# Matrix products of a Strassen-like scheme combined by another chain, with steps on other engines and in a new order

## The chip, the cores and the metric

The kernel runs on one core of one Trainium2 chip. The metric is the device time of one execution in microseconds (us). Five engines matter here: TensorE (in the profile PE, its weight loads PEld), VectorE (DVE), ScalarE (ACT), GpSimd (POOL) and SyncE (SP), which issues every DMA. Each engine works through its own queue in order and waits on semaphores for the others.

## What is computed

An attention read in two directions (tokens read a small state, the state reads the tokens) feeds a two-layer perceptron with softplus between its layers, all in float32:

```python
B, H, S, Ns, D = 8, 8, 512, 32, 64
scores = scale * x @ state^T           # per batch and head
a  = softmax(scores, -1);  xread = a @ state
a2 = softmax(scores^T, -1); sread = a2 @ x
x = concat([xread, sread]) -> (B*(S+Ns), H*D) = (4608, 512)
h = x @ w_in                           # (512, 2048)
g = max(h, 0) + log1p(exp(-abs(h)))    # softplus
out = g @ w_out                        # (2048, 512)
```

## The kernel before

**Rooms.** All tiles come from a few sets of equal buffers, and the profile names a tile after its set: `s` holds 512 words a partition (18 of them), `d` 1024 (14), `g` 2048 (8), `v` small ones, `b` the eight PSUM banks. `W` and `ST` are the first layer's weights and the state.

**Precision.** A float32 product is made of three products of a high and a low part: a step casts the high part (`cast`, on ScalarE, VectorE or GpSimd), a step subtracts it to leave the low part (`elementwise`, on VectorE or GpSimd).

**Blocks.** The work runs batch by batch. Batches 0 and 1 take the plain second product (`gemm2`, step `G`). Batches 2 to 7 and the state's rows (index 8) take a scheme of seven products per block (a 2 by 2 split of both factors). The second-layer weights are therefore combined once into seven slabs and stored to DRAM (steps `N`, `U`, `W`, `Y`, `K`, `j`), and each batch loads 14 slab tiles of 1 MB again (`J`, `slab_load`). For a batch of the scheme the steps are: `v` (state times `W`), `h`, `l` (its high and low part); `Q` (scores); `e`, `f`, `i` (softmax along the tokens), `1` to `7` (softmax along the state, with transposes), `8`, `9` (high and low part of the result); `t`, `u`, `R`, `r`, `y`, `z`, `Z` (the state's read: transpose, copy to SBUF, product, scaling, transpose, high and low part); sixteen times `g` (`gemm1`, six matmuls) and `s` (softplus); `F` (`form_sum`: sums of blocks of the left factor), `H`, `L` (`form_hi`, `form_lo`); fourteen times `M` (`form_product`, line 835; the seven forms in the order of `FORMS`, each in two halves); `k` (`chain`, line 866: adds each finished product from its bank to running sums), `q` (`fold`, halves added) and `P` (`fold_store`).

**Order.** `PLAN` is one character per step, in the order in which the whole program is written out; each engine's queue keeps that order (`Ordered`). `ENG` gives, for those step kinds that may run on several engines, the engine of each occurrence: A is ScalarE, D VectorE, P GpSimd. For the batches 4 and 5 the order repeats.

**What sets the order around the change.** `s_read` (`R`, TensorE) gives a bank that `s_scale` (`r`, line 553, VectorE) multiplies into the small tile `v`; `s_back` (`y`, line 564, TensorE) transposes that. `y` stands in TensorE's queue between two products `M`; all products behind it wait with it. In the repeated block of before, VectorE's queue from the last `g` on holds `F`, `L`, `e`, `k`, `1`, `2`, `3`, `6`, `7` and then `r`.

The lists that name the combination are `FORMS` (line 36), `READS` (832), `CHAIN` (861) and `ENDS` (864). In `CHAIN` an entry without a source is a copy from the bank (`cast`, on ScalarE or VectorE), an entry with one is a VectorE sum of a tile and the bank.

Of the kernel before, what the change touches and what calls it, by code (L numbers as in the profile page):

```python
# [56 lines left out]
ENG = {
    '3': "PPPDPDPDDPDPDPDP",
    '6': "PDPPDPPDDPDPDPDP",
    '8': "APAADDAAADADADADAD",  # L60
    '9': "PPDDDDDDDPDPDPDPDP",
    'D': "PDPAAAADPDPPDAAA",
    'E': "DDDDDDDDDDDPPDDD",
    'F': "DDDDPPDDDDDPDDPPDDDPDDPPDDDPDDPPDDDPDDPPPDDDDDPDDDPDDDPP",
    'H': "PADPAADPAPAAAAAADPDADAADAAAAAADPDADAADAAAAAADPDADAADAAAAAADPDADAADAAADADAAPDPDAAAAPPAAAAAAADADAPAD",
    'I': "ggggggggggdddddg",
    'L': "PDPDPDDDPDPDDDDDDPDPPDDPPDDPDDDPDPPDDPPDDPDDDPDPPDDPPDDPDDDPDPPDDPPDDDDPDPDDDPDDPPDDPDPDPDDPPDPPPP",
    'N': "PPPPDPDPPDPDPDDD",
    'O': "ggggggdgggdggddd",
    'U': "DPPPDDPD",  # L70
    'W': "ADDAAAPD",
    'Y': "DDDDDDPD",
    'h': "AAAAAAAADAAAAAADDDAAAAADAADAAAAAADDAAAAADADAAAAADADAAAAADADAAAAAADAD",
    'k': "AAADADDDDDDDDDDDDDDDDDDAADADDDDDDDDDDDDDDDDDDAADADDDDDDDDDDDDDDDDDDAADADDDDDDDDDDDDDDDDDDAADADDDDDDDDDDDDDDDDDADAADADADDDDDDDDDDDDDDDDDDDDDDDDD",
    'm': "PPPPPPPPPAPPAAPPPPPAAAAPPAPAAAAA",
    'n': "PPDDDPDPDPPPDDPPPDDPDDDDPDPDDDDP",
    'o': "DAADDAAA",
    'q': "PPPPPPPDPDPPPPPDPDPPPPPDPDPPPPPDPDPPPPDDPDDPPPPPPDDD",
    'u': "AAAADDAAAAAAAAAA",
    'w': "AAAAAAAPADPDPDPD",  # L80
    'x': "DPDPPDPDDDPDPDPP",
    'z': "AAAAAAAA",
}


# [58 lines left out]
def attention_then_softplus_mlp(ctx: ExitStack, tc, xn, xt, zq, zp, stk, w_in, w_out, out):  # L144
    nc = Ordered(tc) if PIN else tc.nc
# [571 lines left out]
    def slab_sums():  # L717
        for k in range(NFT // 2):
            w0, w1 = wsum[k], wsum[k + NFT // 2]
            t = slab[k] = r4.take([P, 4, 256], uses=2)  # L720
# [8 lines left out]
            yield
# [255 lines left out]
```

## Time and profile before

| what | value |
|---|---|
| time, median of 3 runs | 688.37 us (688.12 to 688.48) |
| the profiled execution's own time | 689.26 us |
| its span in the trace | 687.5 us |
| granted TensorE clock, mean | 0.967 |
| TensorE busy | 631.7 us |
| VectorE busy | 541.0 us |
| ScalarE busy | 303.4 us |
| GpSimd busy | 335.1 us |

The span is what the trace covers; the times of the views count from its start. A row of a list reads: line, engine, operation, output tile<-input tiles, shape and type, count | busy us, mean ns of one | idle time of the engine before it and what ended it. All steps are recorded by one helper, so every line is L99 and the tiles tell the steps apart.

### The profile page before, as it was taken

How to read it: one execution, taken by the hardware profiler on the slowest of the kernel's cores; microseconds unless marked ns; L12 is line 12 of the kernel's file. 1: busy time of each engine (PE TensorE's matmuls, PEld its weight loads, DVE VectorE, ACT ScalarE, POOL GpSimd, SP SyncE). 2: the span in 40 equal slices, each digit the busy share in tenths (PEclk: the TensorE clock that was granted, in tenths of full speed). 3: DMA queues.
4: the chain of work that ended last, by engine and by line, in shares of the span. 5: the costliest groups of instructions: out<-in, count | busy, mean ns of one | idle time of the engine just before them, and what ended most of it. 6: DMA issues, size and time to landing. Idle time of an engine off the chain costs nothing.

```text
span 687.5 us, 10638 instructions
## 1 busy us (share of the span) xinstructions
PE 631.7 (92%) x4072; PEld 496.7 (72%) x4072; DVE 541.0 (79%) x705; ACT 303.4 (44%) x464; POOL 335.1 (49%) x222
## 2 busy tenths in 40 slices
PE   3798899999999999996999699996999779999897
PEld 1476567678878887885788577784778657898686
DVE  5889969998679965798569965798569966089995
ACT  4798649624284415361354315361255314325110
POOL 2433624794338340873238530773228622079664
PEclk9899999999999999998999989998999989999999
DMA  8987444644542995378708574377807635104654
GB/s 316 406 352 257 107 154 140 223 161 155 197 199 94 417 367 195 132 298 317 295 1 335 224 291 191 122 307 300 297 15 293 259 138 224 68 1 151 217 195 142
DMA packets 48050, 146.96 MB, mean 214 GB/s; under 512 B 4224, under 2 KB 28288, under 8 KB 37248
## 3 DMA queue, kind: packets, MB, share of 16 engines
q1 hardware_dynamic: 48000, 146.29, 57.3%
q8 instruction: 32, 0.52, 0.3%
q14 instruction: 18, 0.15, 0.1%
HBM read 122.68 MB, written 23.59 MB: 213 GB/s over the span
## 4 chain that ended last, share of the span: by engine, by line
PE 62%; DVE 30%; issue 4%; ACT 3%; DMA 1%; SPq 0%; POOL 0%; DVEq 0%; ACTq 0%
PE b L99 62%; DVE d L99 10%; DVE s L99 9%; DVE g L99 6%; DVE v L99 4%; ACT s L99 1%; ACT L99 1%; DMA g<-in_w_in_dram 1%; DVE W L99 1%; ACT d L99 0%; SPq L99 0%; POOL s L99 0%; DVEq L99 0%; ACTq L99 0%
## 5 line engine op out<-in xcount | busy, mean ns | idle before, releaser
L99 PE MATMUL b<-g,d 128*128 128x512 f32 x1344 | 264.0, 351 | 7.4 <-DVE s L99 6.9
L99 PEld LDWEIGHTS b<-g,d 128*128 128x128 f32 x1344 | 214.7, 196 | 51.5 <-issue 14.6
L99 PE MATMUL b<-d,d 128*128 128x512 f32 x768 | 187.6, 397 | 5.3 <-DVE d L99 5.2
L99 PEld LDWEIGHTS b<-d,d 128*128 128x128 f32 x768 | 144.7, 191 | 48.7 <-issue 9.2
L99 PE MATMUL b<-g,s 128*128 128x512 f32 x496 | 126.1, 388 | 4.5 <-ACT g L99 2.7
L99 PEld LDWEIGHTS b<-g,s 128*128 128x128 f32 x496 | 89.5, 191 | 28.6 <-issue 6.1
L99 DVE TENSOR_TENSOR s<-s,b 128x512 f32<-128x512 f32 x117 | 73.2, 680 | 37.9 <-PE b L99 37.9
L99 POOL TENSOR_TENSOR d<-g,d 128x1024 fp32r<-128x1024 f32 x32 | 95.3, 2988 | 9.9 <-DVE d L99 5.0
L99 ACT ACTIVATE g<-b 128x512 f32<-128x512 f32 x96 | 57.2, 598 | 70.5 <-PE b L99 62.1
L99 ACT ACT_TABLE_LOAD x41 | 52.6, 1283 | 49.2 <-DVE v L99 25.3
L99 DVE TENSOR_TENSOR d<-g,d 128x1024 fp32r<-128x1024 f32 x40 | 73.7, 1847 | 0.3
L99 POOL TENSOR_TENSOR s<-s 128x256 f32<-128x256 f32 x37 | 28.6, 791 | 77.1 <-DVE s L99 73.2
L99 ACT CAST d<-b 128x512 fp32r<-128x512 f32 (+2 forms) x52 | 26.8, 558 | 56.8 <-PE b L99 56.8
L99 POOL TENSOR_SCALAR d<-g 128x1024 fp32r<-128x1024 f32 x9 | 13.2, 1468 | 75.3 <-PE b L99 68.8
L99 ACT CAST d<-g 128x1024 fp32r<-128x1024 f32 x39 | 41.0, 1051 | 19.4 <-PE b L99 12.8
L99 POOL TENSOR_TENSOR s<-s,v 128x512 f32<-128x512 f32 x18 | 21.2, 1179 | 55.3 <-DVE v L99 49.0
L99 POOL TENSOR_TENSOR g<-g,g 128x1024 f32<-128x1024 f32 x13 | 35.2, 2708 | 19.9 <-ACT g L99 7.4
L99 PE MATMUL b<-W,ST 64*32 64x512 f32 (+2 forms) x544 | 37.9, 592 | 7.4 <-DVE W L99 4.6
L99 DVE TENSOR_TENSOR d<-b,d 128x512 fp32r<-128x512 f32 (+2 forms) x68 | 41.4, 651 | 1.6 <-ACT d L99 1.5
L99 DVE CAST d<-g 128x1024 fp32r<-128x1024 f32 x24 | 30.5, 1278 | 11.0 <-PE b L99 11.0
L99 POOL TENSOR_SCALAR s<-s 128x512 fp32r<-128x512 f32 x19 | 15.5, 814 | 39.5 <-PE b L99 13.6
L99 DVE TENSOR_TENSOR g<-g 128x1024 f32<-128x1024 f32 x10 | 31.5, 3189 | 0.0
(86 smaller groups left out, 688.9 us busy)
## 6 DMA issues: line engine op xcount, KB each, us to landing
g<-slabs SPq DMA_DIRECT2D x84, 1024.0 KB, 6.9
d<-in_xt_dram SPq DMA_DIRECT2D x16, 512.0 KB, 6.0
d<-in_xn_dram SPq DMA_DIRECT2D x16, 512.0 KB, 5.9
slabs<-d SPq DMA_DIRECT2D x16, 512.0 KB, 2.9
slabs<-g SPq DMA_DIRECT2D x24, 256.0 KB, 5.8
out_dram<-s SPq DMA_DIRECT2D x48, 128.0 KB, 2.0
g<-in_w_in_dram SPq DMA_DIRECT2D x11, 512.0 KB, 9.7
g<-in_w_out_dram SPq DMA_DIRECT2D x11, 512.0 KB, 9.9
```

The source lines that it names most:

```text
L99: return lambda *a, **k: self.tc.keep_in_program_order(f(*a, **k))
```

## The change

The seven products run in another order of forms, and they are combined in another chain. Each half of a batch's rows (index p) had nine sums with a bank and two copies; it has seven sums and one copy. The difference of the form 7, `Sf`, is still made first, but used fifth; one slab changes its sign. The sums of the left factor are made at other forms. The engine lists are new: all 98 `L` are on VectorE (56 before, 42 were on GpSimd), 81 of 98 `H` on ScalarE (60 before), 8 on GpSimd (13 before), 42 of 56 `F` on VectorE (37 before); of `m` and `n`, high and low part of the plain product, 7 and 3 of 32 stay on GpSimd (19 and 14 before); `N`, `U`, `W`, `Y` leave GpSimd but for one `N`. And `PLAN` is another order throughout. In the repeated block, VectorE's and TensorE's steps from the last `g` to `y` were `M H H L F Q M F e e 1 M k 1 k L M i H i 2 2 3 M k k k k L M 5 6 5 t 7 t k M k L 7 M L R k k M r q y` (with copies on ScalarE among the `k`), and are now `M F L Q F M e e L M F 1 1 M H L L M M k k L t q k t M k L L M i i L L R k M k r L 2 2 y`.

```diff
-FORMS = (7, 1, 4, 2, 5, 6, 3)
+FORMS = (1, 2, 6, 5, 7, 3, 4)
 SLAB = {5: 0, 6: 1, 7: 2, 4: 3, 1: 4, 2: 5, 3: 6}
 PLAN = (
...
-    "65t7JLtukMukL67MJHLRJHkkMqrqLPPyM88Jz99ZvJkkMhkhkllMJvJkkMqhkhqPkPkqkqPMlTlPJgJkkqvqsPgPhlhglsgTsgsFvsHghhLgsl"
-    "lgsgsFgsHHgsLgsLgsHFgLsgsgsMsHHHFLFQJHLMFXXeef1MJLk1kfLFMiJHHiw22F3MJkkkkHL34MxJHL5465tJLtwkMukuL67x7wMJHxLRwJ"
...
+    "vsLghhlglsgsgsHgsLgsgFsgsHgsLgsgFsFMsHFLQJFMeHefLMXFJkXkF1f1HMHJHLHFLMJHMHkJkqLPtqJktuPMkHuLLMJHiiLLRHJkMkrL22"
+    "y3MJzL4Z354vJMk6hkhkqkqPlPMlJ5768vJkkMqh7hqPl8Pl9MT9TJgJkkqvqsPgPhlhglsgsgsHvsLghhlglsgsgsHgsLgsgFsgsHgsLgsgFs"
...
 ENG = {
...
-    'D': "PDPAAAADPDPPDAAA",
-    'E': "DDDDDDDDDDDPPDDD",
-    'F': "DDDDPPDDDDDPDDPPDDDPDDPPDDDPDDPPDDDPDDPPPDDDDDPDDDPDDDPP",
-    'H': "PADPAADPAPAAAAAADPDADAADAAAAAADPDADAADAAAAAADPDADAADAAAAAADPDADAADAAADADAAPDPDAAAAPPAAAAAAADADAPAD",
+    'D': "AAPDDAAAAPPDAPAD",
+    'E': "DDDDDDDDDDDDDPDD",
+    'F': "DDDDDDPDDDDDDDPDDDDDDDPPDDDDDDPPDDDDDDPPPDPDDDDDDDDDPPPP",
+    'H': "DAAAAAAAAAAAAAAAAAAADAAAAPAAAAAAAADAAAAPAAAAAAAADAAAAPAAAAAAAADAAAAPAADADDAAADAPAAAAAAAAPAAAPAAAAP",
...
-    'L': "PDPDPDDDPDPDDDDDDPDPPDDPPDDPDDDPDPPDDPPDDPDDDPDPPDDPPDDPDDDPDPPDDPPDDDDPDPDDDPDDPPDDPDPDPDDPPDPPPP",
-    'N': "PPPPDPDPPDPDPDDD",
+    'L': "DDDDDDDDDDDDDDDDDDDDDDDDDDDDDDDDDDDDDDDDDDDDDDDDDDDDDDDDDDDDDDDDDDDDDDDDDDDDDDDDDDDDDDDDDDDDDDDDDD",
+    'N': "DPDDDDDDDDDDDDDD",
...
-    'U': "DPPPDDPD",
+    'U': "DDDDDDDD",
...
-    'm': "PPPPPPPPPAPPAAPPPPPAAAAPPAPAAAAA",
-    'n': "PPDDDPDPDPPPDDPPPDDPDDDDPDPDDDDP",
+    'm': "AAAAAPPADAAPAPPDPAPAAAAAAAAAAAAA",
+    'n': "DDPDDDDDDDDDDPDDPDDDDDDDDDDDDDDD",
...
-            elementwise(t[:, 3], t[:, 1], b21, ALU.subtract, e)
+            elementwise(t[:, 3], b21, t[:, 1], ALU.subtract, e)
...
-            if f in (5, 3):
+            if f in (2, 3):
                 a12, a22 = block(b, 1, c, 0), block(b, 1, c, 1)
-            if f == 7:
+            if f == 1:
                 Sf[b, c] = r2.take([P, 4, 128], uses=2) if b == B else r4.take([P, 4, 256], uses=2)
                 elementwise(Sf[b, c].t, a11, a21, ALU.subtract, engine())
                 TT[b, 0, c].done()
-            elif f == 5:
+            elif f == 2:
                 elementwise(a21, a21, a22, ALU.add, engine())
...
-    READS = {7: 1, 1: 2, 4: 1, 2: 1, 5: 2, 6: 3, 3: 1}
+    READS = {1: 1, 2: 1, 6: 1, 5: 1, 7: 2, 3: 1, 4: 1}
...
-    CHAIN = {7: (("q", None, None),), 1: (("w", None, None), ("q", "q", ALU.add)), 4: (("v", "q", ALU.subtract),),
-             2: (("u", "w", ALU.add),), 5: (("w", "w", ALU.add), ("q", "q", ALU.add)),
-             6: (("v", "v", ALU.add), ("q", "q", ALU.add), ("w", "w", ALU.add)), 3: (("w", "w", ALU.add),)}
-    ENDS = {(2, 0): ("u", 0, 0), (6, 0): ("v", 1, 0), (6, 1): ("q", 1, 1), (3, 0): ("w", 0, 1)}
+    CHAIN = {1: (("m", None),), 2: (("c", "m"),), 6: (("m", "m"),), 5: (("v", "m"),), 7: (("x", "v"), ("m", "m")),
+             3: (("v", "v"),), 4: (("m", "m"),)}
+    ENDS = {(2, 0): ("c", 0, 0), (7, 0): ("x", 1, 1), (3, 0): ("v", 0, 1), (4, 0): ("m", 1, 0)}
...
-                                nc.vector.tensor_tensor(sums[b, p, to].t, sums[b, p, of].t, m.t, op)
+                                nc.vector.tensor_tensor(sums[b, p, to].t, sums[b, p, of].t, m.t, ALU.add)
```

## Rows read from the trace of the kernel before

**Rows 1.** The page, busy time (share of the span) and instructions of each engine.
```profile
PE 631.7 (92%) x4072; PEld 496.7 (72%) x4072; DVE 541.0 (79%) x705; ACT 303.4 (44%) x464; POOL 335.1 (49%) x222
```

**Rows 2.** Waits of TensorE, the longest: us in total, times, longest us.
```profile
PE b L99 <- DVE v L99: 21.1, 4, 5.9
PE b L99 <- DVE s L99: 6.9, 2, 4.2
```

**Rows 3.** Chain that ended last, 390 to 480 us: start, us, what.
```profile
393.97 42.80 PE b L99 x238
...
439.30 6.66 DVE g L99 x2
```

**Rows 4.** Windows, busy us by engine (instructions), then PEclk, DMA share, GB/s.
```profile
399.30:436.80 37.50, 37.50 (x223) 28.12 (x223) 21.90 (x31) 15.23 (x24) 8.25 (x7) 1.00 0.49 188
436.80:471.90 35.10, 29.25 (x236) 24.24 (x235) 33.39 (x41) 14.54 (x21) 23.85 (x11) 0.98 0.70 270
```

**Rows 5.** VectorE's groups by form, 427 to 472 us.
```profile
L99 DVE TENSOR_TENSOR d<-g,d 128x1024 fp32r<-128x1024 f32 x6 | 9.3, 1546 | 0.0
L99 DVE TENSOR_TENSOR g<-g 128x1024 f32<-128x1024 f32 x2 | 6.7, 3408 | 0.0
L99 DVE CAST d<-g 128x1024 fp32r<-128x1024 f32 x4 | 5.0, 1246 | 2.8 <-PE b L99 2.8
L99 DVE TENSOR_TENSOR s<-s,b 128x512 f32<-128x512 f32 x6 | 3.8, 674 | 0.0
...
L99 DVE STREAM_TRANSPOSE s<-b 128x512 f32<-128x512 f32 x2 | 1.4, 706 | 1.4 <-ACT s L99 1.4
...
L99 DVE TENSOR_TENSOR d<-g 128x1024 f32<-128x1024 f32 x1 | 1.2, 1225 | 1.8 <-ACT g L99 1.8
```

**Rows 6.** Timeline of VectorE, 437 to 473 us: start, us, what, count.
```profile
436.79 1.38 DVE L99 CAST d<-g 128x1024 fp32r<-128x1024 f32 x2 [2.76 <-PE b L99]
...
467.50 1.21 DVE L99 TENSOR_TENSOR d<-g,d 128x1024 fp32r<-128x1024 f32 x1
```

**Rows 7.** Windows behind TensorE's five long waits, columns as in Rows 4.
```profile
316.50:321.00 4.50, 4.42 (x16) 3.80 (x17) 3.67 (x5) 0.27 (x1) 4.08 (x3) 0.55 0.68 218
393.97:399.30 5.33, 5.33 (x17) 4.41 (x17) 3.93 (x5) 0.27 (x1) 4.10 (x2) 0.52 0.76 255
471.90:477.20 5.30, 5.30 (x17) 4.39 (x17) 3.89 (x5) 0.27 (x1) 4.09 (x2) 0.50 0.74 255
545.86:550.10 4.24, 4.24 (x14) 3.40 (x14) 4.24 (x6) 1.14 (x2) 4.02 (x3) 0.60 0.61 259
553.74:559.30 5.56, 5.56 (x23) 4.45 (x25) 3.36 (x7) 0.89 (x2) 3.62 (x3) 0.50 0.50 147
```

**Rows 8.** GpSimd's groups by form, 437 to 472 us.
```profile
L99 POOL TENSOR_TENSOR g<-g,g 128x1024 f32<-128x1024 f32 x3 | 8.2, 2733 | 3.3 <-ACT g L99 1.9 <-ACT s L99 1.4
...
L99 POOL TENSOR_TENSOR s<-s 128x256 f32<-128x256 f32 x1 | 0.7, 724 | 4.1 <-DVE s L99 4.1
```

**Rows 9.** The page, costliest groups of the whole execution.
```profile
L99 ACT ACT_TABLE_LOAD x41 | 52.6, 1283 | 49.2 <-DVE v L99 25.3
...
L99 POOL TENSOR_SCALAR d<-g 128x1024 fp32r<-128x1024 f32 x9 | 13.2, 1468 | 75.3 <-PE b L99 68.8
...
L99 ACT CAST d<-g 128x1024 fp32r<-128x1024 f32 x39 | 41.0, 1051 | 19.4 <-PE b L99 12.8
```

**Rows 10.** Windows of the first part, columns as in Rows 4.
```profile
0.00:124.00 124.00, 101.09 (x632) 70.25 (x633) 104.59 (x197) 93.74 (x140) 47.80 (x51) 0.94 0.71 251
124.00:174.00 50.00, 49.55 (x370) 38.17 (x369) 45.92 (x52) 20.58 (x35) 38.02 (x33) 1.00 0.51 172
9.00:35.00 26.00, 17.83 (x122) 10.20 (x123) 23.58 (x55) 20.92 (x45) 11.13 (x11) 0.87 1.04 404
```

**Rows 11.** Window of one whole repeated block, columns as in Rows 4.
```profile
394.70:472.40 77.70, 71.85 (x474) 56.64 (x473) 58.99 (x75) 29.83 (x47) 35.97 (x20) 0.96 0.61 230
```

**Rows 12.** Slab loads issued between 400 and 480 us.
```profile
DMA to landing us min/median/max: 4.8/6.9/12.3
```

**Rows 13.** Timeline of TensorE, 394 to 473 us; here two halves of a form.
```profile
407.21 5.92 PE L99 MATMUL b<-g,d 128*128 128x512 f32 x32
```

More of the change, by code (lines that the diff above doesn't have):

```diff
@@ new lines @@
+    "TSTISTTIIQII1IQ2Ie3OaXbfI1Ic4tO2vuOQ5hhOIla6IbI73aSc88O4e9vOa9Ohh5fatlla6ub7ac88b1919cgblcavbbgIehhlflcAgcAsbt"
+    "XBcgIBICumvCDnDEsEhGmhslsGnmBAIenGOlBfgiCAmigDsCEGDsnaEgbO2OG2a3casGb3bOgacbGBcAcmRsCvnDGBAmTEhmGrAlhnGml4nAg4"
+    "CnDgBTsEjBGCsCDBGjDmEAEgn5aGjsCt65GDujaGEbO6bOgaabOcAGjcsbGccjmBGOmBCAOnvDnjvAEhmChGhlhDAjlGllgEBjnAGsCBTgDCmE"
+    "jgDBTnsEvsCQXihDXihGlmjleEGjefG1n17gXmf7XAjBGn88CsG9j9BGiAmignjDCtsEGDuEjG223g34jGgs5jt6sGu4QojvopNeGNphhefgjl"
+    "olopUgpfm1yjtsWRzKYRZvKrs1njmuvhNGhmlhlhjGllnmgNjrUGsnGmWnKgYGNKsNnGmUgnWNvsNKYGhhlKGmlUmgnWGnsNKYGNKg5GUms6nG"
@@ new lines @@
+    "WmKgYnKGsNGNUmgnWGsKYGmKnNgGsGN7Ug8m79WGnsKG8YmJ9gKNNGsnJmUyGzZWngJYKGsKmGnJgitisGuGgGsGgGsyGz2Z32g34GsG5o6voH"
+    "pogph7hplovlsp4LghghlslgFs5gsH6gs7LgsgFsgsHFgsLgsgsMsHFLMJFFHFMXLHJkXkSHMHJLHLFMJHkkqLPMHJqLPRJHkkvLMHrLhhllMJ"
+    "HLMJkkLLyMJ8z89Z9MJkkqkPkqMPJvJkkMqhqhPlPlMTTJgJkkqvqsPgPhhlglsgsgsHvsLghhlglsgsgsHgsLgsgFsgsHgsLgsgFsFMsHFLQJ"
+    "FMeHefLMXFJkXkF1f1HMHJHLHLMJHkkqLPMHJqLPiitFJtuMkuHkLLMJHLLRJHkkMr223L4yMJz3Z455vJk6Mhkhkqk6PllqMJ7P78899vJkkM"
+    "qhqhPlPlMTTJgJkkqvqsPgPhlhglsgsgsHvsLghhlglsgsgsHgsLgsgFsgsHgsLgsgFsFMsHFLQJFMeHefLMXFJkXkF1f1HMHJHLHFLMJHMHkJ"
@@ new lines @@
+    "kqLPtqJktuPMkHuLLMJHiiLLRHJkMkrL22y3MJzL4Z354vJMk6hkhkqkqPlPMlJ5768vJkkMqh7hqPl8Pl9MT9TJgJkkqvqsPgPhlhglsgsgsH"
+    "vsLghhlglsgsgsHgsLgsgFsgsHgsLgsgFsFMsHFLQJFMeHefLMXFJkXkF1f1HMHJHLHFLMJHMHkJkqLPtqJktuPMkHuLLMJHiiLLRHJkMkrL22"
+    "y3MJzL4Z354vJMk6hkhkqkqPlPMlJ5768vJkkMqh7hqPl8Pl9MT9TJgJkkqvqsPgPhlhglsgsgsHvsLghhlglsgsgsHgsLgsgFsgsHgsLgsgFs"
+    "FMsHFLQJFMeHefLMXFJkXkF1f1HMHJHFLHwMJHkxkMHJLLqtqJtwkPMukHPuLwLMJHxiiLLRHJwkMxrkL2xyMJ2zZ334L4vJkMkhqkhPkqlPwl"
+    "Mx55v6Mh6hkkqlPlqM7P78899vkwgkqhxhPlqwgslwPxgxsgsJgswxvsghhlJglsgsgsJgsgsgsJgsgsgsgsgsgswwxxgswwxxgswwxxgswHHx"
@@ L56 @@
+    "LLgsHHLLgFFsHHLgFLsMFsHHLLFFMJFFFFHMJkkHkLLFFHMJFLHHLHHFLHMJHHkHHkFkLMJqFqPqPHLHMHPLJHkkkLLMJLHHLLLMHJHkkkLLLM"
+    "JLLLMJkkqkPkqkkqMPPMkkqkPqqMPPMkqMPkqkqPP"
 )
 ENG = {
[L58 to L61, printed above, removed]
[L62 to L65 removed]
@@ L75 @@
-    'm': "PPPPPPPPPAPPAAPPPPPAAAAPPAPAAAAA",
-    'n': "PPDDDPDPDPPPDDPPPDDPDDDDPDPDDDDP",
[L77 to L82, printed above, removed]
+    '3': "PPPPPDPDPDPDPDDD",
+    '6': "DDPPDPPDPPPPPPDD",
+    '8': "AAAAAAAAAAAAAAAAAA",
+    '9': "PPPPDDPDDDDDDDDDDD",
+    'D': "AAPDDAAAAPPDAPAD",
+    'E': "DDDDDDDDDDDDDPDD",
+    'F': "DDDDDDPDDDDDDDPDDDDDDDPPDDDDDDPPDDDDDDPPPDPDDDDDDDDDPPPP",
@@ new lines @@
+    'H': "DAAAAAAAAAAAAAAAAAAADAAAAPAAAAAAAADAAAAPAAAAAAAADAAAAPAAAAAAAADAAAAPAADADDAAADAPAAAAAAAAPAAAPAAAAP",
+    'I': "ggggggggggdgdddg",
+    'L': "DDDDDDDDDDDDDDDDDDDDDDDDDDDDDDDDDDDDDDDDDDDDDDDDDDDDDDDDDDDDDDDDDDDDDDDDDDDDDDDDDDDDDDDDDDDDDDDDDD",
+    'N': "DPDDDDDDDDDDDDDD",
+    'O': "gggggddgggddddgg",
+    'U': "DDDDDDDD",
+    'W': "DDAAAAAA",
+    'Y': "DDDDDDDD",
+    'h': "AAAAAAADDAAAAAAAAAAAAAAAAADAAAAAADAAAAAADAAAAAAADAAAAAAADAAAAAAAAAAD",
+    'k': "AADDDDDDDDDDDDDDAADDDDDDDDDDDDDDAADDDDDDDDDDDDDDAADDDDDDDDDDDDDDAADDDDDDDDDDDDDDADADDDDDDDDDDDDDDDDDDDDD",
@@ L83 @@
+    'm': "AAAAAPPADAAPAPPDPAPAAAAAAAAAAAAA",
+    'n': "DDPDDDDDDDDDDPDDPDDDDDDDDDDDDDDD",
+    'o': "DAAADAAA",
+    'q': "PDPPPDPDPDPPPDPDPDPPPPPDPDPPPPPDDDPPPPPPDDDPPPPDDDDD",
+    'u': "AAAADADAAAAAAAAA",
+    'w': "AAAPAAAPPDDDDDDD",
+    'x': "PPPPPDDDDDDDDDDD",
+    'z': "DAAAAAAA",
 }
@@ L871, in chain @@
                         m = prod[(b, p), f]
-                        for n, (to, of, op) in enumerate(CHAIN[f]):
+                        for n, (to, of) in enumerate(CHAIN[f]):
                             if of is None:
```

21 lines of the change are left out of this document (removed).

## The prediction

> **What bounds the kernel now.** First the page: TensorE is busy in 631.7 of 687.5 us [rows 1], so only 55.8 us are idle, and the question is who keeps it waiting. The list of TensorE's waits answers: four waits for the small tile `v` make up 21.1 us, and two for an `s` tile 6.9 [rows 2]; most of the rest lies in the first 110 us. A `v` tile that TensorE waits for is what `s_scale` (`r`) writes and `s_back` (`y`) transposes: one wait per batch, up to 5.9 us. The chain of waits, read in order of time, shows how a batch comes to it: 42.8 us of TensorE without a break, then pieces of VectorE up to `y`, two of them of 6.66 us together [rows 3]. So I looked at the two halves of one batch as windows. In the first, TensorE is busy in all 37.5 us and VectorE in 21.9. In the second, TensorE has 29.25 us of work in 35.1, VectorE is busy for 33.39, and GpSimd for 23.85 [rows 4]. VectorE bounds the second half, and the missing 5.85 us are the wait at `y`.
>
> Why VectorE takes 33 us there is to be seen in its groups: the same shape has several prices. A low part (`L`) of 128x1024 averages 1546 ns, while a single one takes 1.21 us; a block sum in place takes 3408 ns, one into another room 1225; a cast of 128x1024 averages 1246 ns, while two in a row take 1.38 us, 0.69 each. Sums with a bank stay at 674 [rows 5, 6]. The dear ones lie beside GpSimd work. The surplus is 6 x 0.34 + 2 x 2.18 + 4 x 0.56 = 8.6 us, against 23.85 us of GpSimd: 0.36 us lost on VectorE per us of GpSimd.
>
> A wait also costs clock. In the windows right behind the five long waits the granted clock is 0.50 to 0.60 of full speed, the 1.2 GHz level, after TensorE had stood still for 3.6 to 5.9 us; while it works on, it is 1.00 [rows 4, 7]. Length times missing clock gives 2.0 + 2.6 + 2.7 + 1.7 + 2.8 = 11.8 us of lost work [rows 7].
>
> **The change part by part.**
> TensorE gets the same matmuls, so its work stays. What may go is waiting.
>
> *The second half of a batch.* Counted from the new order and engine lists, VectorE does there, up to `r`: nine `L` at 1.21 (10.9), three block sums at 1.23 (3.7), six sums with a bank at 0.674 (4.0), one cast (0.7), two maxima and two transposes at 0.7 (2.8), and some nine small instructions, 1.5 as an estimate from the fold-sized ones: 23.6 us without a neighbour [rows 5, 6]. That is not less than before (33.4 less 8.6 is 24.8): four low parts come over from GpSimd, and the softmax along the state moves behind `y`. What goes is the neighbour. GpSimd keeps two block sums at 2.73, one fold at 0.72 and one cast at 1.47 there, 7.65 us in place of 23.85 [rows 8, 9]. At 0.36 that adds 2.8, and VectorE needs 26.4 us. TensorE needs 29.25, less some 0.7 for the last softplus: 28.5. VectorE is then ready some 2 us ahead of `y`, and the wait at `y` goes. Bounds of the block sums, now mostly on VectorE: 1.23 to 3.41 each; I take the low end, since the two on GpSimd are all that can meet them. An earlier deadline is the second half of form 6: VectorE must have done 11 us of this list (three `L`, three block sums, the softmax's first steps, a cast) by the time that TensorE has done five products and `Q`, 5 x 2.96 + 1 us [rows 13]: 4 us of room.
>
> *The chain.* Seven sums for nine, and one copy for two per index: four VectorE sums (2.7 us) and two ScalarE copies a batch. Most lie in the first half, where VectorE has slack [rows 4]; worth nothing beyond what is counted above.
>
> *Casts on ScalarE.* Three more `H` a batch at 1.05 (3.2 us) [rows 9] beside 29.8 us in 77.7 [rows 11]; ScalarE stays under half busy, so nothing. In the first part 14 more steps move to it (about 0.6 each, an estimate from the large casts, 8.7 us), but the new order changes between softplus and the other functions 36 times instead of 42: six table loads at 1.28 (7.7) less [rows 9]. Even.
>
> *What goes.* The four waits at `y`, 21.1; the two for `s` tiles, 6.9 (one beside a batch's end, one where low parts on GpSimd met the last batch's products); the clock behind five of them, 11.8. Together 39.8 us, which leaves 687.5 - 39.8 = 647.7.
>
> *The first 124 us.* VectorE is busy for 104.6 of them and sets the pace, TensorE for 101.1 [rows 10]. By the lists 25 flexible steps are on GpSimd there instead of 43, and VectorE has 47 instead of 43: about 20 of 47.8 GpSimd us less, 7 us of surplus less at 0.36, 3 us of steps more. I take 2 us of gain. The loads are in a new order, too: two more of `x^T` (512 KB each) now stand ahead of the second piece of `w_in`; at 404 GB/s [rows 10] that is 2.6 us for the products that want that piece. Bounds: 8 us either way.
>
> *124 to 174 us.* TensorE never waits there, VectorE is busy for 45.9 of 50 us and GpSimd for 38 [rows 10]. VectorE now takes 46 flexible steps instead of 33, GpSimd 4 instead of 22. Priced without a neighbour I get 44 to 49 us, about TensorE's own 49.5. This is where VectorE could become late anew: I take 2 us of loss, with 0 to 10 as bounds (the upper end if these steps keep the prices that they had beside GpSimd).
>
> *Left over.* An order written out by hand has small waits somewhere: one us in each of five batches, 0 to 4 each; the last has four more low parts of the weights on GpSimd. Plus 5.
>
> Sum: 647.7 - 2 + 2 + 5 = 652.7 us of span. The median of the runs shown is 0.87 us over the span (688.37 to 687.5), so 653.6.
>
> **The rivals.**
> 1. *GpSimd holds VectorE for the whole of each of its instructions.* Then the 7.65 us [rows 8, 9] count in full: 23.6 + 7.65 = 31.3 against 28.5, a wait of 2.8 us at `y`, plus 2.3 of clock (11.8 over five waits). Five batches give 25, of which 5 are counted; the last has 6 us more GpSimd work: 654 + 26 = 680. For it: in-place sums at 3408 [rows 5], a free one plus almost a GpSimd one. Against it: all dear instructions together lost only 0.36 per us. The Trainium skill ("SBUF — State Buffer", section "Who interferes with whom") states this rule: the pair of ports that VectorE and GpSimd share is an exclusive lock for whole instructions when VectorE has two SBUF inputs or runs in a 2-port mode. By it the sum is rival 1's; the rows agree for single instructions, and disagree with it as a price for every GpSimd us.
> 2. *VectorE becomes late in the first 174 us*, at the upper bounds: 8 + 10 in place of 0: 18 us more would be 672, half of it 663; I write 668. For it: VectorE's share there is already the highest of the kernel [rows 10].
> 3. *Slab loads become the wait, and the kernel slower.* A batch moves 230 GB/s x 77.7 us = 17.9 MB [rows 11]; without the waits it has 69.5 us, so 257 GB/s. Only four slab rooms are free, and a product takes 2.96 us [rows 13]: a load must land 3 x 2.96 = 8.9 us after its room is free. It lands in 6.9 at the median and 12.3 at worst [rows 12]. Each turn of four rooms costs what the landing has over 8.9; with 2.5 turns a batch and 5.4 batches' worth, 34.7 us are given back, and the kernel becomes slower, from an overall landing of 11.5 on. At 12.3 everywhere: 654 + 46 = 700. Against it: TensorE has no wait for a slab now, and DMA reached 404 GB/s [rows 10].
> 4. *The change doesn't do what it says:* `r` stands behind as much VectorE work as before, and the waits at `y` stay as they are: 688. Against it is the count above.
>
> **How the numbers follow.** The forecast, 646 to 662, gets 0.66; rival 1 0.12 (680), rival 2 0.10 (668), rival 3 0.07 (700), rival 4 0.03 (688), and 0.02 go to less than 640. The predicted time is 654. The range reaches down to 640 (no new wait and the first part's best bound: 647.7 - 8) and up to 682, past rivals 1 and 2. About 0.2% (1.4 us) is what a measurement of this kernel can tell from no change: faster by more 0.90, within 0.03, slower 0.07.
>
> **What would show it.** TensorE's waits should list `v` with under 4 us in all, and the page a granted clock near 1 behind 120 us. In a repeated block's second half GpSimd should be busy for about 8 us, the 128x1024 low parts should average near 1.25 us, and VectorE have idle time that ends with TensorE. Two transposes `y` should lie 70 us apart, not 77.7. Rival 1 would show as `v` waits of about 3 us with low parts above 2 us; rival 2 as waits for `s` or `d` tiles before 174 us; rival 3 as waits of PE for DMA `g<-slabs`. The prediction is wrong if a wait that isn't in the list of before, of 5 us or more per batch, takes the place of the one at `y`.

## The result and the profile after

The changed kernel takes 634.67 us (median of four runs, 634.05 to 634.82) against 688.25 for the kernel before (median of four): a ratio of 0.922, interval 0.9205 to 0.9237. The direction was forecast; the time lies 5.3 us below the low end of the range. The profiled execution took 634.05 us, its span 632.3. Of the 55 us of span that are gone, 40.8 lie where the prediction put its 39.8, behind 242 us; it was the two stretches ahead that gave 14.5 where it expected nothing.

The page's first line, to be held against [rows 1]: TensorE is busy in 97% of the span, and GpSimd does 123 us in place of 335.

```profile
PE 613.6 (97%) x4072; PEld 485.3 (77%) x4072; DVE 486.6 (77%) x741; ACT 326.8 (52%) x497; POOL 123.0 (19%) x108
...
L99 ACT ACT_TABLE_LOAD x35 | 44.9, 1283 | 2.3 <-DVE v L99 1.7
```

All of TensorE's waits (us in total, times, longest). No `v` tile is among them, where [rows 2] had 21.1 us, and no slab. All of them lie in the first 53 us:

```profile
PE b L99 <- DMA ST<-in_zp_dram: 5.0, 1, 5.0
PE b L99 <- ACT s L99: 3.3, 2, 1.9
PE b L99 <- DVE W L99: 2.7, 2, 2.0
PE b L99 <- ACT d L99: 1.8, 1, 1.8
PE b L99 <- DMA d<-in_xt_dram: 0.7, 1, 0.7
PE b L99 <- DVE g L99: 0.7, 2, 0.4
PE b L99 <- POOL d L99: 0.2, 1, 0.2
```

The chain that ended last, between 355 and 440 us, is one piece, where [rows 3] showed 42.8 us of TensorE and then VectorE up to `y`:

```profile
354.94 85.17 PE b L99 x632
```

Windows of one repeated block, `y` to `y` (columns as in [rows 4]): the two halves, and the second up to the end of `r` alone; then the whole block ([rows 11]) and the first two stretches ([rows 10]).

```profile
365.70:406.60 40.90, 40.90 (x243) 30.89 (x242) 24.92 (x37) 19.48 (x31) 6.06 (x8) 1.00 0.55 211
406.60:435.30 28.70, 28.70 (x235) 24.06 (x233) 27.62 (x35) 14.43 (x19) 8.30 (x5) 1.00 0.83 323
...
406.60:432.75 26.15, 26.15 (x219) 21.85 (x218) 25.07 (x32) 14.43 (x19) 7.55 (x4) 1.00 0.81 313
...
365.70:435.30 69.60, 69.60 (x477) 54.96 (x475) 52.54 (x72) 33.91 (x50) 14.36 (x13) 1.00 0.67 257
0.00:111.10 111.10, 96.69 (x630) 67.28 (x631) 95.83 (x202) 91.59 (x148) 25.16 (x32) 1.00 0.77 278
111.10:159.10 48.00, 48.00 (x368) 37.96 (x367) 46.71 (x83) 23.90 (x39) 4.57 (x4) 1.00 0.56 182
```

In the windows that begin at 0 the clock can read too high: the trace's first entry on it lies at 16.8 us before and at 25.9 us after, and what is ahead of it counts as 1.00. The last section shows what the matmuls tell there.

The second half shows TensorE without a gap, VectorE still busy in 27.62 of 28.7 us, and `r` done at 432.75, 2.5 us ahead of `y` at 435.3. It is the same in three of the four batches that waited. In the last one GpSimd has 14.30 us of work in the half, and `r` ends only 0.06 us ahead of `y`: there the wait is gone, and no slack is left.

```profile
476.20:504.90 28.70, 28.70 (x233) 23.84 (x231) 27.75 (x32) 15.99 (x22) 14.30 (x8) 1.00 0.85 325
```

VectorE's groups by form around it (395 to 435 us, columns as in [rows 5]): eleven low parts in place of six, and a block sum in place at 1217 ns instead of 3408.

```profile
L99 DVE TENSOR_TENSOR d<-g,d 128x1024 fp32r<-128x1024 f32 x11 | 14.9, 1366 | 7.2 <-ACT d L99 7.2
L99 DVE TENSOR_TENSOR s<-s,b 128x512 f32<-128x512 f32 x6 | 3.8, 675 | 0.0
...
L99 DVE TENSOR_TENSOR g<-g 128x1024 f32<-128x1024 f32 x2 | 2.4, 1217 | 0.0
...
L99 DVE CAST d<-g 128x1024 fp32r<-128x1024 f32 x1 | 2.0, 2042 | 0.0
```

The slab loads issued between 360 and 440 us ([rows 12] for before):

```profile
DMA to landing us min/median/max: 4.9/9.2/12.6
```

Where the 55 us went, by the starts of the eight transposes `y` in the two timelines (us from the mark before):

| mark | before | after | less |
|---|---|---|---|
| first `y` | 123.8 | 111.1 | 12.7 |
| second | 49.8 | 48.0 | 1.8 |
| third, fourth | 17.0, 51.9 | 17.0, 51.9 | 0 |
| fifth | 74.1 | 68.1 | 6.0 |
| sixth | 77.4 | 69.5 | 7.9 |
| seventh | 77.9 | 69.6 | 8.3 |
| eighth | 81.9 | 69.7 | 12.2 |
| end | 133.8 | 127.4 | 6.4 |

### The profile page after: what moved, and what is told of

It reads as the page before. It is cut to its first block, busy times and chain, and to the rows that moved or that the text cites. A ratio compares the mean times of both kernels' runs of the same rounds, so it can differ in the third digit from the quotient of the medians.

```text
span 632.3 us, 10553 instructions
## 1 busy us (share of the span) xinstructions
PE 613.6 (97%) x4072; PEld 485.3 (77%) x4072; DVE 486.6 (77%) x741; ACT 326.8 (52%) x497; POOL 123.0 (19%) x108
## 4 chain that ended last, share of the span: by engine, by line
PE 83%; DVE 1%; ACT 1%; issue 0%
PE b L99 83%; DVE s L99 1%; DVE d L99 1%; ACT L99 0%; ACT s L99 0%; DVE g L99 0%; ACT d L99 0%
## 5 line engine op out<-in xcount | busy, mean ns | idle before, releaser
L99 PE MATMUL b<-g,d 128*128 128x512 f32 x1344 | 252.1, 340 | 0.1
L99 DVE TENSOR_TENSOR d<-g,d 128x1024 fp32r<-128x1024 f32 x72 | 99.0, 1388 | 44.9 <-ACT d L99 44.5
L99 ACT ACTIVATE g<-b 128x512 f32<-128x512 f32 x96 | 57.0, 597 | 77.9 <-PE b L99 77.8
L99 ACT CAST d<-g 128x1024 fp32r<-128x1024 f32 x59 | 61.2, 1050 | 33.7 <-PE b L99 16.3
L99 DVE TENSOR_TENSOR s<-s,b 128x512 f32<-128x512 f32 x91 | 57.4, 677 | 27.2 <-PE b L99 27.2
L99 POOL TENSOR_TENSOR g<-g,g 128x1024 f32<-128x1024 f32 x10 | 25.9, 2592 | 141.6 <-DVE g L99 81.8
L99 ACT ACT_TABLE_LOAD x35 | 44.9, 1283 | 2.3 <-DVE v L99 1.7
L99 DVE TENSOR_TENSOR d<-d,d 128x1024 fp32r<-128x1024 f32 (+1 forms) x22 | 27.1, 1243 | 1.0 <-ACT d L99 0.9
L99 ACT ACTIVATE s<-b 128x512 f32<-128x512 f32 x32 | 18.6, 599 | 14.2 <-PE b L99 14.0
L99 ACT COPY s<-b 128x512 f32<-128x512 f32 x32 | 17.8, 589 | 14.8 <-PE b L99 14.6
L99 ACT CAST d<-d 128x1024 fp32r<-128x1024 f32 x18 | 18.8, 1048 | 10.6 <-DVE d L99 8.0
L99 DVE TENSOR_TENSOR s<-s,s 128x512 fp32r<-128x512 f32 x31 | 21.8, 709 | 2.4 <-ACT s L99 2.4
```

The costliest lines, as they stand in the source:

```text
L99: return lambda *a, **k: self.tc.keep_in_program_order(f(*a, **k))
```

## The experiments: the steady batches

The theory on record says that the neighbour, GpSimd, made VectorE late at `y`, and that taking its work away is what removes the wait. The rival is the order: `r` stood behind the softmax along the state, whoever worked beside it. The engine lists and the order can be changed one without the other.

**Low parts back on GpSimd, in the changed kernel.**

```diff
-    'L': "DDDDDDDDDD...",   # 98 on VectorE
+    'L': "PDPDPDDDPDPDDDDDDPDPPDDPPDDPDDDP...",   # the list of before: 42 on GpSimd
```

> The kernel after with the list L of before: 42 of the 98 low parts back on GpSimd, nothing else. Theory A (waits at y came from VectorE beside GpSimd): VectorE's second half of a batch loses four low parts (4.8 us) and gains 0.36 to 0.44 us for each of some 13 us of added GpSimd (5 us), while GpSimd's own low parts of 2.4 to 3.4 us stand in the chain to the products: waits of 0 to 4 us per batch, time 636 to 660. Rival B (the order alone removed the waits): 634 to 636, no wait of TensorE behind 35 us. If the port lock counted in full: waits of 6 us or more at y per batch, time above 665.

640.26 us, 0.9285 to 0.9312 of before: 5.6 us more than the change. The time lies low in theory A's wide range and above the 634 to 636 of rival B, so by itself it decides little. But GpSimd is as busy in the half as it was before, and still there is no wait of more than 1.3 us. The second half of a block:

```profile
411.30:440.10 28.80, 28.40 (x231) 23.55 (x230) 25.09 (x27) 14.12 (x19) 22.99 (x9) 1.00 0.77 286
```

GpSimd 22.99 us here and 23.85 in [rows 4]; the wait at `y` is gone in one and 5.85 us long in the other. The two kernels differ in order, forms, chain and the other lists; the next runs change one of these at a time.

**The same list the other way, in the kernel before.** All 98 `L` on VectorE, nothing else.

```diff
-    'L': "PDPDPDDDPDPDDDDDDPDPPDDPPDDPDDDP...",
+    'L': "DDDDDDDDDD...",
```

> The kernel before, its order and chain kept, with all 98 low parts on VectorE. Theory A: in the second half of a batch GpSimd loses 13 us and VectorE gets 4.8 us of low parts and loses 5 us of surplus: VectorE 33.4 to 33 us, the wait at y shrinks only a little unless block sums become cheaper too; I expect 660 to 685 us. Rival B (the order alone decides): the waits at y stay at 5.8 us, 686 to 692. Rival C (the engine list alone decides): the waits at y vanish, 648 to 655.

685.86 us, 0.9943 to 0.9975: some 3 us less, just between the ranges of theory A and rival B. The waits at `y` are not shorter but longer, 6.3 to 6.4 us in the three steady batches. The gain lies elsewhere: the wait of 2.7 us for an `s` tile at 650 us is gone, and from the eighth `y` to the end it takes 129.7 us in place of 133.8. TensorE's wait for `v`, and the second half:

```profile
PE b L99 <- DVE v L99: 23.5, 4, 6.4
```

```profile
437.25:472.90 35.65, 29.26 (x236) 24.25 (x235) 33.98 (x45) 14.45 (x21) 11.38 (x6) 0.98 0.64 252
```

GpSimd's work is halved and VectorE's stays at 34 us: the instructions that got cheaper (low parts at 1370 ns, block sums in place at 2313) only made room for the low parts that came over. So the list of the low parts does not remove the wait in the old order. The other lists were left as they were in this run.

**The order alone, in the kernel before.** The steps 2 to 9 of the softmax along the state go behind `r` in the three batches that repeat, all but `2` behind `y` too; forms, chain and the engine of each step kind stay.

```diff
-    ...HHi22F3MJkkkkHL34M5JHL465t7JLtukMukL67MJHLRJHkkMqrqLPPyM88Jz99ZvJkkMhkhkllMJvJkkMqhkhq...
+    ...HHiFMJkkkkHLMJHLtJLtukMukLMJHLRJHkkMqrqL22PPy3MJz4Z354vJkkM6hkhk5llM7J68vJkk7Mq8hk9hq9...
```

> The kernel before with one change of order: in the three repeated batches the softmax along the state (2, 3, 4, 5, 6, 7, twice each) and its high and low parts stand behind the transpose y, as in the kernel after, not ahead of the scaling r. Engines and chain are those of before. Theory C (the order decides: these steps put 7 to 8 us of VectorE work ahead of r, dear ones beside GpSimd included): the three waits of 5.8 us at y vanish, VectorE's second half falls from 33.4 to about 26 us, and 3 x (5.8 + 2.4 of clock) = 25 us go: 662 to 668. Theory A (GpSimd beside VectorE decides): the waits shrink by half at most, 674 to 684. Rival: another wait takes their place, 686 to 690.

664.62 us, 0.9635 to 0.9679. `y` to `y` is 68.1, 69.5 and 69.6 us: those of the changed kernel to the tenth. `r` is done 1.3 to 1.4 us ahead of `y`. Windows of the second half up to the end of `r` and up to `y`; the one up to the end of `r` in the kernel before; and VectorE's groups by form from 410 us to that `y`:

```profile
420.70:448.03 27.33, 27.33 (x226) 22.86 (x225) 25.80 (x29) 13.00 (x18) 21.36 (x9) 1.00 0.77 299
420.70:449.40 28.70, 28.70 (x234) 24.04 (x233) 27.17 (x31) 13.00 (x18) 22.73 (x9) 1.00 0.79 305
```

```profile
436.80:471.65 34.85, 29.23 (x235) 24.22 (x233) 33.14 (x40) 14.54 (x21) 23.60 (x10) 0.99 0.70 272
```

```profile
L99 DVE TENSOR_TENSOR d<-g,d 128x1024 fp32r<-128x1024 f32 x6 | 9.3, 1558 | 0.0
L99 DVE TENSOR_TENSOR g<-g 128x1024 f32<-128x1024 f32 x2 | 6.7, 3408 | 0.0
L99 DVE CAST d<-g 128x1024 fp32r<-128x1024 f32 x4 | 5.0, 1246 | 2.8 <-PE b L99 2.8
```

These are the dear prices of [rows 5], within 12 ns: the neighbour is there in full, and `r` is in time. What left the queue ahead of `r` is the softmax, 7.3 us of VectorE (33.14 to 25.80). That settles the three steady batches.

**The order alone, in all four batches that wait for `v`.** The last one, too; there the steps `w` and `x` (high and low part of `W`, for the state's rows) had to move later with it.

> The kernel before with the softmax along the state moved behind y in VectorE's queue, now in all four batches that wait for it (the last batch too, where the steps of w and x of the fourth batch move later with it). Theory of the order: the last batch's two waits before y (4.2 and 3.6 us, at 545 and 553 us) go as those of the other three went, y to y of that batch falls from 81.9 to 69.6 to 72 us, and the time to 652 to 656 us. Rival, that the last batch's waits come from its fewer rooms for other work and stay in part: y to y 75 to 82 us, time 658 to 665 us.

654.64 us, 0.9488 to 0.9518. The last batch falls from 81.9 to 69.5 us, `r` 0.55 us ahead of `y`. No `v` is left among TensorE's waits, with 20.63 us of GpSimd in its second half:

```profile
490.60:519.40 28.80, 28.80 (x234) 24.12 (x233) 27.16 (x30) 11.94 (x17) 20.63 (x7) 1.00 0.77 303
```

A new order of a few softmax steps gives 34 of the 54 us, with the chain, the lists and the first part of before.

**The chain of nine sums again, in the changed kernel.** The sums of forms 2 and 5 and the copies are issued twice, with the same result.

```diff
...
-    nc.vector.tensor_tensor(sums[b, p, to].t, sums[b, p, of].t, m.t, ALU.add)
+    for _ in range(2 if f in (2, 5) else 1):
+        nc.vector.tensor_tensor(sums[b, p, to].t, sums[b, p, of].t, m.t, ALU.add)
```

> The kernel after with nine sums and two copies per index again: the sums of forms 2 and 5 and the copy of form 1 are made twice, with the same result. All four extra sums of a batch (2.7 us of VectorE) lie ahead of r, where r is done 2.5 us before y. Theory (seven sums are worth what slack they buy): waits of 0 to 1 us per batch, 634.5 to 639. Rival (VectorE sets the pace of a batch): 2.7 us x 6.5 batches = 18, time 650 to 653.

639.04 us, 0.9272 to 0.9305: 4.4 us more. `r` ends 0.06 to 0.4 us ahead of `y`, no longer 2.5, and `v` is back among the waits with 2.0 us in all, 1.3 of them in the last batch, which had no slack. The slack that the shorter chain leaves is used nearly to its end.

**How much slack VectorE has.** The low parts of forms 5 and 6 are made twice, with the same result.

> The kernel after with the low parts of forms 5 and 6 made twice, with the same result: four more VectorE instructions of 1.2 us per batch (4.7 us) ahead of r. By the account of the second half (27.6 us busy of 28.65, r done 2.5 us before y) 3.6 us fit, and 1 to 2.2 us of wait come per batch, TensorE waiting for v or d: 640 to 648. Rival (all hidden): 634 to 636. Rival (no slack, all on the path): 4.7 x 6.5 = 31, time 660 to 668.

656.29 us, 0.9517 to 0.9551: 21.6 us more, a miss. `y` to `y` is 2.3 to 5.4 us longer in each of the four batches, most in the last one, which had no slack, and the waits are spread over three kinds of tile:

```profile
PE b L99 <- DVE v L99: 6.4, 4, 2.3
PE b L99 <- DVE d L99: 5.5, 7, 2.2
...
PE b L99 <- DVE s L99: 1.6, 1, 1.6
```

The slack of 2.5 us at `y` is not the only one: all seven waits for a `d` tile end with a low part, which a product wants soon after it is made, and each product that comes late is a wait of its own.

## The experiments: the first part

Here the forecast was 2 us of gain, and 12.7 came. The first `y` is the mark. TensorE's waits up to it, in the kernel before:

```profile
PE b L99 <- DMA ST<-in_zp_dram: 4.9, 1, 4.9
PE b L99 <- DVE d L99: 4.8, 2, 3.5
PE b L99 <- DVE W L99: 4.6, 2, 2.4
PE b L99 <- ACT d L99: 2.9, 2, 2.7
PE b L99 <- ACT g L99: 2.7, 1, 2.7
PE b L99 <- DVE g L99: 1.8, 4, 0.9
PE b L99 <- DMA d<-in_xt_dram: 1.2, 1, 1.2
```

22.9 us against 14.4 after, 8.5 of the 12.7. The rest is TensorE's own busy time, 100.89 us up to that mark against 96.69. Both changes lie behind the first loads: up to 33 us TensorE waits for 13.6 us before and 13.9 after, behind that for 9.3 and 0.4. After two of these later waits in the kernel before (2.7 us for `g`, up to 55.8 us, and 3.5 us for `d`, up to 87.2) the granted clock falls to half:

```profile
57.70:61.20 3.50, 3.50 (x10) 2.68 (x10) 3.50 (x5) 3.50 (x7) 1.59 (x1) 0.51 1.08 390
88.50:91.90 3.40, 3.40 (x10) 2.63 (x9) 1.74 (x3) 2.23 (x3) 0.00 (x0) 0.50 0.73 248
```

That is 3.4 us of lost work, and the changed kernel has no such fall behind 26 us. The stretches behind 35 us, before and after:

```profile
35.00:123.80 88.80, 80.85 (x478) 59.38 (x477) 78.76 (x138) 71.12 (x95) 34.77 (x33) 0.96 0.61 207
35.00:111.10 76.10, 75.59 (x471) 56.17 (x470) 68.65 (x141) 69.73 (x101) 19.36 (x20) 1.00 0.68 238
```

So waits and the clock behind them are 11.9 of the 12.7 us, as in the batches. What shortened the waits is the question of the runs that follow.

**The order of the first loads.** The changed kernel with two loads of `x^T` behind two pieces of `w_in`, as before; the order of the first loads is then that of before but for one load of the state.

```diff
-    "TSTISTTIIQII1IQ2I...",
+    "TSTISIITTQII1IQ2I...",
```

> The kernel after with the first loads in the order of before: the two loads of x^T of batch 1 behind the second and third piece of w_in, all else kept. Theory (the order of loads is a small part of the first part): the second product with W starts 1 to 3 us earlier (16.0 to about 14), the scores of batch 1 later, first y within 2 us of 111.1, time 633 to 637. Rival (the order of loads brought the gain): first y at 117 or later, time above 640.

635.01 us, 0.9215 to 0.9242; first `y` at 111.8, as in a second trace of the changed kernel. The loads' order, one of the prediction's worries, costs and gives nothing that shows.

**The engine lists of the first part.** First the old lists in the new order; then the new lists in the old order; then of these only the lists that divide work between GpSimd and VectorE (3, 6, 9, E and n).

> The kernel after, its order and all else kept, but the steps ahead of the first transpose y take the engines that before gave the same occurrences (3, 6, 8, 9, D, E, m, n, h, u, o): 41 of them on GpSimd instead of 24. Theory A (the first part gained 12.7 us, 123.8 to 111.1 us, because VectorE lost less time beside GpSimd, and because TensorE kept its clock without long waits): most of the gain goes, first y near 119 to 124 us, time near 643 to 648 us, VectorE's int32 shifts (TENSOR_SCALAR) back from 455 to 600 ns or more. Rival B (the gain comes from the new order of steps and loads): first y stays near 111 to 113 us, time 635 to 637.

> The kernel before, its order kept, with the engines of after for the occurrences ahead of the first y: GpSimd does 24 of these steps instead of 41. Theory A (less GpSimd beside VectorE makes the first part short): first y from 123.8 to 112 to 117 us, time 677 to 682. Rival B (order): first y stays at 121 to 124, time 685 to 688.

> The kernel before; ahead of the first y only the steps that leave GpSimd for VectorE move (lists 3, 6, 9, E, n as in after), no cast moves to ScalarE, which keeps its work and its 30 table loads of the first part. Theory D (moving casts to ScalarE made the kernel with all early lists slower, since ScalarE there was busy for 98.7 of 126.7 us): first y at 118 to 122 us, 2 to 5 us faster than before, 683 to 687. Rival (VectorE is the engine that is late, and gets more work): first y at 124 to 127, time 688 to 692.

| first `y`, us | lists of before | lists of after |
|---|---|---|
| order of before | 123.8 | 126.7 |
| order of after | 117.9 | 111.1 |

The times are 641.96, 692.16 and 686.54 us (0.9304 to 0.9337, 1.0037 to 1.0066, 0.9961 to 0.9986 of before). Each mark is read from one trace; a second trace of the changed kernel has 111.8. The third run came as its theory had it; the first two did not: 117.9 lies between the two ranges given, and 126.7 above both. The new order gives 5.9 us with the old lists. The new lists cost 2.9 us in the old order and give 6.8 in the new one; the lists of GpSimd and VectorE alone give 2.4 in the old order (first `y` at 121.4), so it is the others, most of which move steps to ScalarE, that cost there. The windows up to the first `y`, old lists in the new order, and new lists in the old order:

```profile
0.00:117.90 117.90, 98.20 (x631) 68.54 (x632) 103.31 (x195) 86.30 (x134) 45.55 (x47) 0.94 0.73 261
```

```profile
0.00:126.70 126.70, 102.17 (x631) 70.09 (x632) 97.97 (x196) 98.65 (x151) 30.15 (x34) 0.97 0.69 245
```

With the old lists VectorE is the busiest (103.31), with the new lists in the old order ScalarE is (98.65), with 29 table loads of 1283 ns before the mark. The new order has 24, with either lists. That ScalarE has the room for what the new lists give it only there is an argument so far; the runs with table loads added and taken away test it. What in the new order gives its own 5.9 us was not taken apart further, but the loads' order is not it.

**The new first part ahead of the old rest.**

> All steps up to the first y in the order and on the engines of after, all steps behind in the order, on the engines and in the chain of before. Theory (the first part stands by itself): first y at 111 to 112 us instead of 123.8, the waits at y as before, time 688.4 - 12.7 = 675 to 677. Rival (the gain of the first part is paid back by steps that it leaves for later, VectorE being busy for 46 of 50 us there): 680 to 688.

679.17 us, 0.9856 to 0.9884: 9.2 us of the 12.7, between the ranges of theory and rival. The first `y` comes at 112.2, and behind it a wait of 2.7 us shows at 121 us, where the old rest follows on the new order.

**Table loads added.** Three tiny softplus calls among other functions, which bring six more table loads, 30 before the first `y`.

```diff
+            if k in (7, 10):
+                nc.scalar.activation(probe, probe, AF.Softplus)
```

> The kernel after with three tiny softplus calls on a tile of one column, each between two calls of the other table, so that ScalarE loads a table six times more in the first part: 30 as before instead of 24, 7.7 us plus some 0.6 us for the calls. Theory E (fewer table loads gave ScalarE the room for the casts that left GpSimd): first y 4 to 8 us later, 115 to 119, time 638 to 643. Rival (ScalarE has slack there): first y at 111 to 113, time 634 to 637.

639.87 us, 0.9283 to 0.9309: 5.2 us more; first `y` at 116.4, ScalarE gets 6 x 1.283 + 3 x 0.2 = 8.3 us of work more. It has so little slack in this part that 4.6 to 5.3 of the 8.3 us arrive at TensorE, by the two traces of the changed kernel (111.8 and 111.1). That is most of the 6.8 us that the new lists give in this order.

**Table loads taken away.** Two steps moved ahead of one softplus, two ahead of another (`a` and `A`, in which ScalarE takes the upper half of a weight of `w_in` or `w_out` from its stored words; the texts on record call them low-part and copy steps): 20 loads in place of 24 before the first `y`, all the four behind 33 us. The first of these runs stood without the changed kernel beside it; the two that follow share a chip.

```diff
-...OG2a3casGb3bOgacbGBcAcmRsC...   ...CnDgBTsEjBGCsCDBGjDmEAEgn5aGjsC...
+...OG2a3caaAsGb3bOgcbGBccmRsC...   ...CnDgBTAasEjBGCsCDBGjDmEEgn5GjsC...
```

> The changed kernel with four of ScalarE's table loads less in the first part (two low-part and copy steps moved ahead of one softplus, two ahead of another), 20 in place of 24 before the first y. Theory that the loads set the length of the first part: each load is 1283 ns, and 8.3 us of added loads and work cost 5.3 us, so four less give back 0.64 x 5.1 = 3.3 us at most: first y at 108 to 110 us in place of 111.1, time 631 to 634 us. Rival, that ScalarE's slack in this part is used up only when more is added: first y 110.5 to 111.5, time 634 to 636 us.

> The changed kernel itself, so that the next one is timed on the same chip beside it: 634 to 635 us, first y at 111 us, TensorE's waits of the first part 14.4 us in all and none behind 33 us.

> The changed kernel with four table loads less, all of them behind 33 us, beside the changed kernel. TensorE of the changed kernel waits in its first part only before 33 us. Theory that a load costs only where TensorE waits or the granted clock falls: no difference beyond 0.2%, 633.0 to 635.5 us, first y at 110.5 to 111.5 us, with ScalarE some 5 us less busy before it. Rival, that the loads set the pace of the first part: 1.5 to 3.3 us faster, first y at 108 to 109.6 us.

633.58 us in the first run (0.9187 to 0.9212 of before). Side by side: 633.68 us (633.15 to 634.04) against 635.42 (634.96 to 635.96) for the changed kernel, so 1.7 us or 0.27%, with ranges that don't meet. The first `y` moves by 1.3 us, from 111.8 to 110.5. The theory of no difference beyond 0.2% missed, though its range holds the first `y`. The rival's 1.5 to 3.3 us hold the 1.7, but its 108 to 109.6 don't hold the first `y`, and the trace doesn't show loads that pace the whole part. TensorE's timeline shows the one place, 16 matmuls of a product with `W`, in the changed kernel, with four loads less, and with six more:

```profile
48.86 2.08 PE L99 MATMUL b<-W,ST 64*32 64x512 f32 x16
```

```profile
49.24 1.09 PE L99 MATMUL b<-W,ST 64*32 64x512 f32 x16
```

```profile
49.30 1.81 PE L99 MATMUL b<-W,ST 64*32 64x512 f32 x12
52.74 1.05 PE L99 MATMUL b<-W,ST 64*32 64x512 f32 x4 [1.63 <-DVE W L99]
```

The same 16 matmuls take 1.09 us with nothing to wait for. In the changed kernel they take 2.08, and the list of waits is silent: pauses shorter than a matmul's own record count as busy. They want `W` columns that VectorE makes from ScalarE's output, and in the changed kernel VectorE waits for that output just there:

```profile
48.72 1.11 DVE L99 SCALAR_TENSOR_TENSOR W<-s,s 128x512 int32<-128x512 int32 x1 [0.94 <-ACT s L99]
```

ScalarE has three loads around this point (at 44.8, 46.7 and 49.8 us), and two with four loads less (46.3 and 49.2). By the starts of the same matmuls in both kernels, the lead made here is 1.3 us (0.4 us behind at matmul 260, 1.0 ahead at 320) and changes by 0.3 in the rest of this part: the other loads are hidden. With six loads more, 2.1 us of the lag are made at the same place and most of the rest near 60 and 85 us. The version with four loads less is the fastest of the study.

## Why the prediction was right, and where it failed

- **The waits at `y`, the `s` tiles and the clock behind them (39.8 us):** right in size. From the fourth `y` to the end the marks give 6.0 + 7.9 + 8.3 + 12.2 + 6.4 = 40.8 us.
- **VectorE's count of the second half:** right. Up to the end of `r` it is busy for 25.07 us where 26.4 were summed, `r` is 2.5 us ahead of `y` where 2 were forecast, and `y` to `y` is 69.5 to 69.7 where 70 were. The price of 0.36 us per us of GpSimd was in part luck. Beside GpSimd's 8.3 us eleven low parts and one cast lost 11 x 0.156 + 1.35 = 3.1 us against the 1.21 and 0.69 of [rows 6], which is 0.37; with the fold (1261 ns beside 408 in the run with only the order changed) it is 3.9 us, 0.47. Two of the signs failed: the low parts average 1366 ns and not 1250, and VectorE's idle time around this half (7.2 us) ends with ScalarE's high parts, not with TensorE.
- **The cause:** half right. The prediction counted that the softmax moves behind `y`, and called the neighbour what goes. The two are separate: order without lists removes the wait with GpSimd at 22.7 us, the list of the low parts without order leaves it at 6.4. The sum came out because it counted everything that stands ahead of `r`; its word on which entry decides was an argument, and the runs overturned it. Of the two waits for `s` tiles, the one at 650 us does go when the low parts leave GpSimd, as it said; the other, at 546 us, goes with the order.
- **The first 124 us (2 of gain, 8 either way):** the step that failed, by 10.7 us. It took VectorE's share as the pace and netted moved steps against a cheaper neighbour, 7 less and 3 more, and took half of that. VectorE's busy time up to the mark fell by 8.6 us (104.39 to 95.83), so already this term was too small. And TensorE's waits were never summed as in the batches: 9.3 us of them lie behind 33 us, with 3.4 us of clock lost behind two of them, and nearly all of that went. The runs put 5.9 us on the new order and 6.8 on the new lists in it. ScalarE was rightly called even (93.54 to 91.59 us), but it has little room: its six table loads, put back, take 4.6 to 5.3 us again, and the same lists in the old order, with 29 loads, cost 2.9.
- **124 to 174 us (2 of loss):** 1.8 of gain. The upper bound, that VectorE's steps there keep their prices beside GpSimd, did not come: VectorE is busy for 46.71 of 48.0 us, and TensorE has no recorded wait. By the starts of the same matmuls 1.1 of the 1.8 us lie at products with `W`, in pauses too short for the list, and 0.4 in a wait at 131 us that the prediction passed over. With the old early lists in the new order the stretch takes 49.8 us again, but for another reason, a wait of 1.5 us for `sreadT` that neither kernel has; which part of the change gives the 1.8 us stays open.
- **Left over (5 of loss):** 0.1. Behind 53 us TensorE has no recorded wait at all. No row stood behind this term.
- The misses, 10.7 + 3.8 + 4.9 and 1.0 of the first term, are the 20.4 us between 652.7 and 632.3. The low end of the range (647.7 - 8 = 639.7 of span) has no new waits and the first part's best bound; it is passed by 7.4 us, some 4.7 of them in the first part, 1.8 in the stretch behind it and 1.0 in the first term.
- **Rival 1 (the lock counts in full)** did not come. The Trainium skill ("SBUF — State Buffer", section "Who interferes with whom") has the ports that VectorE and GpSimd share as an exclusive lock, so that one instruction is held while the other has them. Single rows agree: a low part of 2203 ns starts at 412.43 us, its GpSimd neighbour ends at 413.55, and 1.08 us are left from there. What does not hold is the price that rival 1 made of it, every GpSimd us in full: 3.9 us are lost beside 8.3 of GpSimd, and 22.7 us of GpSimd make no late `r`.
- **Rival 2** (VectorE late in the first 174 us) and **rival 4** did not come. Lists without their order do lengthen the first part, to 126.7 us, but there ScalarE is the busiest engine, not VectorE.
- **Rival 3 (slab loads):** the rate came as forecast (257 GB/s a block, 323 in the second half) and the landing grew from 6.9 to 9.2 us, past the 8.9 that the prediction took as the point of harm. No wait for a slab followed, so that point was set too low. Which landing time would hurt wasn't tried; the nearest sign is one wait of 1.3 us for a slab with the low parts on GpSimd.

## What to carry to other kernels

When a wait ends with an engine that works through a queue, list everything that stands ahead of the awaited instruction and ask first which of it could stand behind; moving work that nobody awaits yet gave 34 us here with no instruction made cheaper, and moving low parts to another engine some 3 (685.86 against 688.85). What engine lists are worth depends on the order: the same lists cost 2.9 us in one order and gave 6.8 in the other. Sum the waits and the missing clock of every stretch, the first one too, before a reserve is set on it.

## What was not expected of the hardware

- Behind 26 us the granted clock of the changed kernel is 1.00 in every window shown, where the kernel before fell to half behind each long wait [rows 7]. Ahead of that a reading of 1.00 can be empty. In the run with four loads less, five matmuls of 128x512 take 2.50 us in a stretch at 0.50; in the changed kernel beside it the same five take the same 2.50 us in a stretch that reads 1.00, where its trace has no entry on the clock yet:

```profile
22.77 2.50 PE L99 MATMUL b<-d,d 128*128 128x512 f32 x5 [0.19 <-POOL d L99]
23.10:25.00 1.90, 1.90 (x5) 1.16 (x4) 1.90 (x5) 0.33 (x1) 0.30 (x1) 0.50 1.02 403
```

```profile
22.52 2.50 PE L99 MATMUL b<-d,d 128*128 128x512 f32 x5 [0.19 <-POOL d L99]
23.10:25.00 1.90, 1.90 (x12) 1.04 (x14) 1.90 (x6) 0.69 (x1) 0.06 (x1) 1.00 1.02 405
```

  Such matmuls start 0.43 us apart there and 0.23 apart behind 29 us in both. So TensorE runs at the lower level, 1.2 GHz, in both, whatever the windows read.
- The list of waits can miss a pause of 1 us that falls between matmuls shorter than their own records; comparing the start of the same matmul in two kernels finds it.
- DMA moved 323 GB/s through a half block with a median landing of 9.2 us for 1 MB, and TensorE did not wait for one load of it.
